# A float32 first block, and the first two blocks in one written-out order

## The chip, the core and the metric

One core of a Trainium2 chip runs the kernel. The metric is the device time of one execution in microseconds. Its engines are named as the profile names them: PE (TensorE, the matrix products), DVE (VectorE), ACT (ScalarE), POOL (GpSimd) and SP, whose queue issues nearly all DMAs.

## What is computed

A convolution with weights made for each position, then a feed-forward layer. `x` is [4, 4096, 192] float32, `weight_gen` [4, 4096, 8, 7] float32; `w_in` [192, 2048] and `w_out` [2048, 192] arrive as float64.

```python
w = softmax(weight_gen, axis=-1)
out = einsum('bshk,bskhg->bshg', w, x_unf)   # 7 taps: rows s-6 .. s
h = out.reshape(16384, 192) @ w_in
g = h * (1.0 / (1.0 + exp(-1.702 * h)))
result = (g @ w_out).astype(float32)
```

## The kernel before

**Tiles.** The 16384 rows are 32 blocks of 512 (`NB`, four tiles of 128 rows), and the 2048 columns of `w_in` are 16 slices of 128 (`NF`). One block and one slice are a **unit**; 512 units run in order. A unit's first products (`whole`, L386, and `halves`, L396) make `h` of 128 columns by 512 rows in one bank of PSUM, its gate (`gate`, L406: Tanh on ACT, a multiply on DVE) makes `g`, `split` (L412) makes two float16 parts of `g` on ACT and DVE, and its second products (`second`, L418) add to the block's output in PSUM, which `store` (L430) writes out.

**Precision.** Everything that goes into a product is split in a high and a low float16 part, so that a float32 product becomes several float16 ones: four of 512 columns in `whole`, half of one in `halves` (only 64 of the 192 inputs are left for it, so two units share the array, one in each half of its rows), and three of 192 columns for each of four row tiles in `second`. The parts need a power of two as a scale for each block (`scales`, L224) and one for each weight (`bound_in`, L343, and `bound_out`, L348), which come from the largest sum of absolute values.

**Weights.** They arrive as float64 and are narrowed to float32 in place (`narrow`, L318), 512 columns at a time: two ACT steps (bits of the low word, L326, and the exponent, L329), two DVE steps (L332, L333), and one ACT pass for the absolute sums (L337). The float32 value then stands in the high word of each 64-bit element, so it is read with a step of two words. Key `i` is the upper 128 rows of `w_in`, `t` the other 64 (two halves stacked on the partitions), `o` is `w_out`. Once a scale is there, `parts_in`, `parts_tail` and `parts_out` (L362 to L378) make the high part on ACT (L358), the low part on DVE (L360), and eight small DMAs copy the tail's high part to `th_` (L373).

**The convolution.** For the first block, `attend_first` (L169) makes seven taps and three sums on DVE, and PE turns the four results by products with an identity and adds them up in two banks of PSUM (L182, float32 products). `scales(0)` and `split_first` (L258) go from there. For all other blocks POOL makes taps and sums (`attend`, L153), DVE and ACT split (`split_x`, L271), and a DMA transposes (`turn`, L282). `hold` (L478) is a small copy on POOL that makes it wait for a DVE result.

**Order.** Every engine and queue takes its instructions in the order in which they are written. `plan` (L459) gives each step of the side work a due number counted in units, negative ahead of the first; the loop at L581 goes through the units in groups: first two, then 85 groups of six (`sixes`), and calls what is due between the units. Within a six, three units get `whole` first and three after `halves`, and the second products of the six before are spread between them (`seconds`, L563). Banks `h0` to `h5` go around by the unit's number (`bank`, L383); the four remaining uses (top sums, exponents, warm-up products, turned taps) share them. All loads are issued on SP's queue at the start (L483 to L495).

## Time and profile before

| | |
|---|---|
| median of 3 runs | 1084.66 us (1083.29 to 1085.37) |
| span of the profiled execution, first to last instruction | 1082.0 us; its own time is given by this span alone |
| PE busy | 1047.2 us, 97% of the span |
| DVE, ACT, POOL busy | 875.3, 702.7 and 721.9 us |
| mean granted PE clock | 0.984 of full speed |

Lnn is a line of the kernel above. "x" counts instructions; a float32 product stands as two records. A busy PE says only that a product was under way. Waits of engines off the path cost nothing by themselves.

### The profile page before, as it was taken

How to read it: one execution, taken by the hardware profiler on the slowest of the kernel's cores; microseconds unless marked ns; L12 is line 12 of the kernel's file. 1: busy time of each engine (PE TensorE's matmuls, PEld its weight loads, DVE VectorE, ACT ScalarE, POOL GpSimd, SP SyncE). 2: the span in 40 equal slices, each digit the busy share in tenths (PEclk: the TensorE clock that was granted, in tenths of full speed). 3: DMA queues.
4: the chain of work that ended last, by engine and by line, in shares of the span. 5: the costliest groups of instructions: out<-in, count | busy, mean ns of one | idle time of the engine just before them, and what ended most of it. 6: DMA issues, size and time to landing. Idle time of an engine off the chain costs nothing.

```text
span 1082.0 us, 22229 instructions
## 1 busy us (share of the span) xinstructions
PE 1047.2 (97%) x8821; PEld 734.4 (68%) x8821; DVE 875.3 (81%) x1558; ACT 702.7 (65%) x1251; POOL 721.9 (67%) x484
## 2 busy tenths in 40 slices
PE   5589999999999999999999999999999999999998
PEld 4156767777777767776776677667766777676766
DVE  8877878888797888878788887978887787789765
ACT  5866766666666666666666666656676666667665
POOL 4449858677855868686587868568776856886100
PEclk9689999999999999999999999999999999999999
DMA  9300220313012121301212120121212102101010
GB/s 303 128 18 17 47 78 18 92 33 93 16 36 82 25 92 33 89 18 33 78 34 92 32 84 24 33 78 32 90 36 75 33 18 92 33 22 41 18 33 16
DMA packets 73519, 60.71 MB, mean 56 GB/s; under 512 B 60620, under 2 KB 66252, under 8 KB 71880
## 3 DMA queue, kind: packets, MB, share of 16 engines
q1 hardware_dynamic: 73128, 59.11, 18.9%
q8 instruction: 69, 1.13, 0.4%
q14 instruction: 34, 0.28, 0.1%
q10 hardware_dynamic: 288, 0.20, 0.1%
HBM read 31.96 MB, written 12.58 MB: 41 GB/s over the span
## 4 chain that ended last, share of the span: by engine, by line
PE 94%; DVE 3%; ACT 2%; issue 1%; DMA 1%; SPq 0%; ACTq 0%
PE o L426 17%; PE o L428 16%; PE o L427 16%; PE h L391 10%; PE h L392 10%; PE h L393 10%; PE h L394 10%; PE h L403 6%; DMA xb<-in_x_dram 1%; DVE tap L149 0%; ACT abs L337 0%; DVE g L416 0%; ACT bits L326 0%; DVE h L410 0%; DVE m L332 0%
## 5 line engine op out<-in xcount | busy, mean ns | idle before, releaser
L426 PE MATMUL o<-wos,g 128*128 128x192 f16 x2048 | 505.4, 247 | 0.1
L428 PE MATMUL o<-woh,g 128*128 128x192 f16 x2048 | 504.7, 246 | 0.0
L427 PE MATMUL o<-wol,g 128*128 128x192 f16 x2048 | 504.7, 246 | 0.0
L410 DVE SCALAR_TENSOR_TENSOR h<-th,h 128x512 f32<-128x512 f32 x512 | 347.0, 693 | 177.9 <-ACT th L409 170.3
L409 ACT ACTIVATE th<-h,s 128x512 f32<-128x512 f32 x512 | 343.3, 687 | 219.1 <-PE h L404 125.2
L416 DVE SCALAR_TENSOR_TENSOR g<-g,h 128x512 f16<-128x512 f16 x512 | 349.4, 682 | 13.2 <-ACT g L415 1.2
L164 POOL TENSOR_TENSOR acc<-acc,prod 128x768 f32<-128x768 f32 x186 | 344.6, 1853 | 14.6
L415 ACT ACTIVATE g<-h 128x512 f16<-128x512 f32 x512 | 306.0, 598 | 46.2 <-DVE h L410 46.2
L149 POOL TENSOR_TENSOR prod<-xb,wb 128x768 f32<-128x768 f32 x186 | 291.7, 1568 | 11.1
L426 PEld LDWEIGHTS <-g 128*128 128x128 f16 x2048 | 200.5, 98 | 75.5 <-issue 35.6
L427 PEld LDWEIGHTS <-g 128*128 128x128 f16 x2048 | 200.7, 98 | 36.4
L428 PEld LDWEIGHTS <-g 128*128 128x128 f16 x2048 | 200.7, 98 | 0.1
L393 PE MATMUL h<-xt,w0h 128*128 128x512 f16 x512 | 195.1, 381 | 0.0
L391 PE MATMUL h<-xt,w0l 128*128 128x512 f16 x512 | 195.0, 381 | 0.0
L394 PE MATMUL h<-xt,wth 128*128 128x512 f16 x512 | 195.0, 381 | 0.0
L392 PE MATMUL h<-xt,w0h 128*128 128x512 f16 x512 | 195.0, 381 | 0.0
L143 POOL TENSOR_TENSOR wb<-wb,wr 128x224 f32<-128x224 f32 x31 | 17.9, 577 | 217.8 <-DVE wr L140 214.9
L278 DVE SCALAR_TENSOR_TENSOR xs<-acc,s,xs 128x512 f16<-128x512 f32 (+1 forms) x62 | 92.8, 1536 | 0.0
L393 PEld LDWEIGHTS <-w0h 128*128 128x128 f16 x512 | 50.3, 98 | 61.0 <-issue 1.1
L394 PEld LDWEIGHTS <-wth 128*128 128x128 f16 x512 | 50.3, 98 | 61.0 <-issue 1.0
L403 PE MATMUL h<-xt,tl 64*128 64x512 f16 x256 | 70.9, 382 | 2.3 <-DVE g L416 2.3
L404 PE MATMUL h<-xd,tl 64*128 64x512 f16 x256 | 71.1, 382 | 0.5 <-DVE g L416 0.5
(94 smaller groups left out, 526.2 us busy)
## 6 DMA issues: line engine op xcount, KB each, us to landing
xb<-in_x_dram SPq DMA_DIRECT2D x12, 1344.0 KB, 6.4
out_dram<-osb SPq DMA_DIRECT2D x31, 384.0 KB, 2.4
wb<-in_weight_gen_dram SPq DMA_DIRECT2D x16, 224.0 KB, 3.2
ro<-in_moe_w_out_dram SPq DMA_DIRECT2D x4, 768.0 KB, 12.3
xb<-in_x_dram SPq DMA_DIRECT2D x3, 768.0 KB, 6.2
ri<-in_moe_w_in_dram SPq DMA_DIRECT2D x4, 512.0 KB, 8.7
...
```

Source lines behind the costliest of these rows:

```text
L164: nc.gpsimd.tensor_tensor(acc, acc, t, ALU.add)
L391: nc.tensor.matmul(ps, lhsT=w0l[:, s], rhs=x0, start=start, stop=False)
L392: nc.tensor.matmul(ps, lhsT=w0h[:, s], rhs=x2, start=False, stop=False)
L393: nc.tensor.matmul(ps, lhsT=w0h[:, s], rhs=x0, start=False, stop=False)
L394: nc.tensor.matmul(ps, lhsT=th_[:, s], rhs=x1, start=False, stop=stop)
L409: nc.scalar.activation(t, hp[u], AF.Tanh, scale=scale[u[0]][:, 4:5])
L410: nc.vector.scalar_tensor_tensor(hp[u], t, 1.0, hp[u], ALU.add, ALU.mult)
L415: nc.scalar.activation(g[:, 0], hp[u], AF.Copy, scale=2.0**-12)
L416: nc.vector.scalar_tensor_tensor(g[:, 1], g[:, 0], -(2.0**12), hp.pop(u), ALU.mult, ALU.add)
L426: nc.tensor.matmul(o, lhsT=lo, rhs=wos[:, d], start=a and j % 2 == 0, stop=False, skip_group_check=True)
L427: nc.tensor.matmul(o, lhsT=hi, rhs=wol[:, d], start=False, stop=False, skip_group_check=True)
L428: nc.tensor.matmul(o, lhsT=hi, rhs=woh[:, d], start=False, stop=z, skip_group_check=True)
```

## The change

The loads, their order, and everything from the third block on (its sixes, due numbers and banks relative to the six) stay as they are. Changed is what lies ahead of it:

- **Block 0 in float32.** The turned first block is copied to SBUF as float32 (`keep`, ACT and DVE). `whole` becomes one float32 product with the narrowed weights, `halves` two of half height, `second` one for each row tile, with the narrowed `w_out` as its moving operand. `gate` writes float32 `g` to SBUF; `split` is not called for this block, and neither its scale nor its parts are made.
- **Taps of block 0.** Five on DVE, two on POOL (`dtap`, `ptap`), two sums on DVE, and five results turned (`tr`) instead of four. Both subtractions of the softmaxes 0 and 1 are on POOL. The warm-up has 11 products instead of 7; the one in front of the first products (5, float16) is gone.
- **Weights' scales and parts** are made while block 0 runs, in pieces of 1024 columns for bits, absolute sums and parts (key ending in `w`); four DMAs instead of eight copy the tail's high part.
- **One list.** All steps of the first 32 units stand in `ORDER`, which is written out as read; each name is one step of one of the functions. `W` is `whole`, `X` the half products of a group of four units, `gt` and `gm` the two steps of a gate, `gh` and `gl` those of a split, `S` the second products (a, b: two row tiles), `nb nm n1 n2 na` narrowing and sums, `ph pl ps pd` the parts, `sN.k` softmax, `aN.k` attention, `cN xN tuN` scales, split and turn of block N, `hold` POOL's waits. The units use four banks; `h4` and `h5` are left to exponents and tops. The sixes start at unit 32; units 28 to 31 get their second products in the first of them.

```diff
 ONE = float(1 << 23)
+
+ORDER = """
+warm.11 s1.0 s0.0 s1.1 s0.1 s0.2 s0.3 s0.4 s0.5 s0.6 s0.7 ptap.1 dtap.5 dtap.2 tr.5 ptap.3 dtap.6 dtap.4
+tr.6 sum.2.3 nm.i0 dtap.0 tr.2 nm.i1 sum.0.1 s1.2 nb.i0 nb.t0 tr.0 n1.i0 n2.i0 s1.3 nm.t0 tr.4 nb.i1 n1.t0
+s1.4 s1.5 n2.t0 s1.6 keep.0 keep.2 a1.0 keep.1 W.0 n1.i1 nb.i2w W.1 n2.i1 a1.1 na.i0w X.0 nm.o0 a1.1p nm.i2
+n1.i2 W.2 gt.0 a1.2 gm.0 nb.o0w W.4 gt.1 n1.o0 a1.2p W.3 gt.2 gm.1 n2.o0 W.5 gm.2 nm.o1 a1.3 S.0a gt.3 n1.o1
+S.0b nb.t1 gm.3 a1.3p n2.i2 X.1 n2.o1 s3.0 s2.0 s2.1 S.1b gt.5 a1.4 W.6 nm.t1 gm.5 nm.i3 W.7 s2.2 a1.4p gt.6
+s2.3 S.1a s2.4 gm.6 gt.7 W.9 gm.7 gt.4 s3.1 S.2 a1.5 gm.4 s3.2 na.o0w n1.i3 W.8 n1.t1 nb.o2w a1.5p S.3 n2.t1
+s3.3 na.t0w n2.i3 X.2 a1.6 s2.5 na.i2w s3.4 S.4 a1.6p nm.o2 s3.5 nm.o3 n1.o2 gt.8 W.11 n2.o2 gt.9 s2.6 lp2
+gm.8 S.5 a2.0 c1.0 gt.11 nm.o4 W.10 nb.o4w gm.11 a2.1 S.6 gm.9 n1.o4 gt.10 s3.6 W.13 n2.o4 a2.1p S.7 gm.10
+n1.o3 W.12 n2.o3 a2.2 bin.0 nm.o5 c1.1 S.8 na.o2w n1.o5 a2.2p c1.2 X.3 n2.o5 x1.0 x1.1 bin.1 S.9 gt.12 x1.2
+bin.2 tu1 W.14 ph.t0w cg1 gm.12 W.15 gt.13 pl.t0w pd.t0w S.10 ph.i0w s4.0 ph.i2w gm.13 s4.1 S.11 pl.i0w
+gt.15 xd1 s4.2 S.12 na.o4w pl.i2w gt.14 gm.15 W.16 hold.A a2.3 gm.14 W.17 bout.0 a2.3p X.4 s4.3 bout.1 W.18
+gt.17 bout.2 gt.16 W.19 a2.4 ph.o2w gm.16 S.13 gm.17 gh.16 co1 a2.4p gh.17 ps.o2w S.14a gl.17 S.14b gl.16
+ph.o0w S.15a S.15b pl.o0w ps.o0w W.20 st.a pl.o2w st.b S.16a gt.18 S.16b gt.19 S.17a hold.B gm.18 a2.5 S.17b
+gm.19 gh.18 W.21 gh.19 gl.18 a2.5p ph.o4w gl.19 S.18 ps.o4w X.5 pl.o4w W.22 gt.20 gt.21 a2.6 gm.20 W.23
+gm.21 gh.20 S.19 gh.21 gl.20 a2.6p gt.23 W.24 gt.22 gm.23 S.20 gl.21 gh.23 hold.C a3.0 gm.22 W.25 gl.23
+gh.22 S.21 s4.4 gl.22 a3.1 c2.0 X.6 W.27 gt.25 a3.1p gt.24 gm.25 W.26 gm.24 gh.25 c2.1 S.22 a3.2 gh.24 gl.25
+gt.27 c2.2 W.29 gt.26 co2 a3.2p cg2 S.23 x2.0 gl.24 gm.27 W.28 gm.26 gh.27 a3.3 S.24 gh.26 gl.27 gl.26 S.25
+x2.2 x2.1 X.7 s4.5 tu2 S.26 s4.6 gt.28 a3.3p gt.29 gm.28 W.31 gm.29 gh.28 W.30 gt.31 gl.28 a3.4 S.27 gh.29
+gm.31 gl.29 gh.31 a3.4p gt.30 gl.31 xd2 gm.30 gh.30 a3.5 gl.30 a3.5p a3.6 a3.6p
+"""
+TURNED = [a for a in ORDER.split() if a.startswith("tr.")]
...
+    def softmax(blk, eng=nc.gpsimd):
...
+        if blk == 0:
+            near["w"], near["r"] = w, r
+            return
+        yield
...
+    def weights_near(by):
...
+        if by == "dve":
+            near[by] = ps_h.tile([P, N], F32, tag="h0", name="w")[:, 0 : J * H * K].rearrange("p (n k) -> p n k", k=K)
+            nc.vector.tensor_tensor(near[by], near["w"], near["r"], ALU.mult)
+        else:
+            near[by] = x32[1][:, 0 : J * H * K].rearrange("p (n k) -> p n k", k=K)
+            nc.gpsimd.tensor_tensor(near[by], near["w"], near["r"], ALU.mult)
...
+    turned, taps, added = [], {}, []
...
+    def first_tap(k, by):
+        if k < K - 2:
...
+        taps[k] = t
+        tap(0, {"dve": nc.vector, "pool": nc.gpsimd}[by], t, k, near[by])
+
+    def add_taps(k, l):
+        nc.vector.tensor_tensor(taps[k], taps[k], taps[l], ALU.add)
...
+    def turn_tap(k):
...
+        for ps, c, n in zip(turned, (0, P), (P, C1)):
+            for j in range(J):
+                nc.tensor.matmul(
+                    ps[:n, j * P : (j + 1) * P], lhsT=taps[k][:, j, c : c + n], rhs=ident,
+                    start=start and j == 0, stop=stop, skip_group_check=True,
+                )
...
-    def split_first():
...
-        nc.scalar.activation(x1[0:C1], b[0:C1], AF.Copy, scale=s[0:C1])
-        xd[0] = tpool.tile([P, J, P], F16, tag="xd", name="xd")
-        nc.scalar.activation(xd[0][C1:P], b[0:C1], AF.Copy, scale=s[0:C1])
-        yield
-        nc.vector.scalar_tensor_tensor(x2, a, s, x0, ALU.mult, ALU.subtract)
-        nc.vector.scalar_tensor_tensor(x1[C1:P], b[0:C1], s[0:C1], x1[0:C1], ALU.mult, ALU.subtract)
+    x32 = [const.tile([P, N], F32, name=f"x32{c}") for c in range(2)]
+
+    def keep(n):
+
+
+        if n == 2:
+            nc.vector.tensor_copy(x32[1][C1:P], turned[1][0:C1])
+        else:
+            p = (P, C1)[n]
+            nc.scalar.copy(x32[n][0:p], turned[n][0:p])
...
-    def narrow(key, a, at):
...
-        nc.scalar.activation(b, low_u, AF.Relu, bias=third, scale=2.0**-29 * (1 - 2.0**-10))
-        ring = (ps_o, "o") if at % 2 else (ps_h, f"h{4 + at // 2 % 2}")
-        m = ring[0].tile([P, QC], F32, tag=ring[1], name="m")
-        nc.scalar.activation(m, f, AF.Copy, scale=2.0**-112)
-        yield
-        m = m.bitcast(I32)
-        nc.vector.scalar_tensor_tensor(m, m, 3, b, ALU.logical_shift_left, ALU.bitwise_or)
-        nc.vector.scalar_tensor_tensor(high, high, -(1 << 31), m, ALU.bitwise_and, ALU.bitwise_or)
-        yield
-
-        t = stage.tile([P, QC], BF16, tag="abs", name="abs", bufs=1)
-        nc.scalar.activation(t, f, AF.Abs, accum_out=sums[:, at : at + 1])
...
+    narrowed = {k: words(v, F32)[1] for k, v in raw.items()}
+    bits, exps = {}, {}
+    spares = itertools.cycle(("h4", "h5"))
...
+    def narrow(step, key):
...
+        k, s = cols_of(key)
+        n = s.stop - s.start
+        if step == "nb":
+            low_u, _ = words(raw[k][:, s], U32)
+            b = stage.tile([P, n], I32, tag=f"b{n}", name="bits", bufs=2)
+            nc.scalar.activation(b, low_u, AF.Relu, bias=third, scale=2.0**-29 * (1 - 2.0**-10))
+            for i in range(n // QC):
+                bits[k, s.start // QC + i] = b[:, i * QC : (i + 1) * QC]
+            return
+        if step == "na":
...
+            one = {"t": 0, "i": 1, "o": 3}[k] + s.start // (2 * QC)
+            nc.scalar.activation(wos[:, 0:n].bitcast(BF16), narrowed[k][:, s], AF.Abs, accum_out=sums[:, one : one + 1])
+            return
+        at = k, s.start // QC
+        if step == "nm":
+            m = ps_h.tile([P, QC], F32, tag=spare(), name="m")
+            nc.scalar.activation(m, narrowed[k][:, s], AF.Copy, scale=2.0**-112)
+            exps[at] = m.bitcast(I32)
+        elif step == "n1":
+            m = exps[at]
+            nc.vector.scalar_tensor_tensor(m, m, 3, bits.pop(at), ALU.logical_shift_left, ALU.bitwise_or)
+        else:
+            _, high = words(raw[k][:, s], I32)
+            nc.vector.scalar_tensor_tensor(high, high, -(1 << 31), exps.pop(at), ALU.bitwise_and, ALU.bitwise_or)
...
-        yield from bound(0, 6, e, "h3")
+        yield from bound(0, 3, e, spare)
...
-        yield from bound(6, 12, e, "o")
+        yield from bound(3, 6, e, spare)
...
-
-    def parts_in(c):
-        s = slice(c * QC, (c + 1) * QC)
-        yield from parts_of(("i", c), to_in, w0h[:, s], w0l[:, s])
-
-    def parts_tail(c):
...
+    def parts(step, key):
+
+
+        kind, s = cols_of(key)
+        f, to = narrowed[kind][:, s], to_out if kind == "o" else to_in
+        hi, lo = (t[:, s] for t in {"i": (w0h, w0l), "o": (woh, wol), "t": tail}[kind])
+        if step == "ph":
+            nc.scalar.activation(hi, f, AF.Copy, scale=to)
+        elif step == "pl":
+            nc.vector.scalar_tensor_tensor(lo, f, to, hi, ALU.mult, ALU.subtract)
+        elif step == "ps":
+            nc.scalar.activation(wos[:, s], hi, AF.Copy, scale=2.0**-12)
+        else:
+            for p0 in (0, C1):
+                to = th_[p0 : p0 + C1, 2 * s.start : 2 * s.stop].rearrange("d (q two k) -> two d q k", two=2, k=P)
+                for h in range(2):
+                    nc.sync.dma_start(to[h], hi[h * C1 : (h + 1) * C1].rearrange("d (q k) -> d q k", k=P))
...
     def bank(u):
-        hp[u] = ps_h.tile([P, N], F32, tag=f"h{(u[0] * NF + u[1]) % Q}", name="h")
+        n = u[0] * NF + u[1]
+        hp[u] = ps_h.tile([P, N], F32, tag=f"h{n % 4 if n < few else (n - few) % Q}", name="h")
...
     def whole(u, start, stop):
 
         blk, f = u
+        if blk == 0:
+            w = narrowed["i"][:, f * P : (f + 1) * P]
+            nc.tensor.matmul(hp[u], lhsT=w, rhs=x32[0], start=start, stop=stop)
+            return
...
         blk, f = u
+        if blk == 0:
+            w = narrowed["t"][:, f // 2 * P : (f // 2 + 1) * P]
+            nc.tensor.matmul(hp[u], lhsT=w[0:C1], rhs=x32[1][0:C1], start=not last_u, stop=last_u)
+            nc.tensor.matmul(hp[v], lhsT=w[C1:P], rhs=x32[1][C1:P], start=not last_v, stop=last_v)
+            return
...
     def gate(u):
 
-        t = gpool.tile([P, N], F32, tag="th", name="th", bufs=2)
-        nc.scalar.activation(t, hp[u], AF.Tanh, scale=scale[u[0]][:, 4:5])
-        nc.vector.scalar_tensor_tensor(hp[u], t, 1.0, hp[u], ALU.add, ALU.mult)
+        th[u] = t = gpool.tile([P, N], F32, tag="th", name="th", bufs=2)
+        nc.scalar.activation(t, hp[u], AF.Tanh, scale=scale[u[0]][:, 4:5] if u[0] else SIG / 2)
+        yield
+        to = hp[u]
+        if u[0] == 0:
+            to = gg[u] = gpool.tile([P, N], F32, tag="g", name="g32")
+        nc.vector.scalar_tensor_tensor(to, th.pop(u), 1.0, hp[u], ALU.add, ALU.mult)
...
     def second(u, j):
...
+        if blk == 0:
+            w = narrowed["o"][:, d]
+            nc.tensor.matmul(o, lhsT=g[:, s], rhs=w, start=a and j % 2 == 0, stop=z, skip_group_check=True)
+            return
...
-        o, s = po.pop((blk, i)), scale[blk][:, 5:6]
+        o, s = po.pop((blk, i)), scale[blk][:, 5:6] if blk else 0.5
...
-    few = len(units) % Q
+    few = 2 * NF
...
-        plan((-36.1, -35.7, -35.1, -34.6, -33.6), softmax(0, V, w_first))
...
-        plan((-36.2,), once(warm, 7, ident, P))
-        plan((-32.1, -30.4, -27.7, -25.0), attend_first(w_first))
-        plan((-24.9, -24, -23, -22, -21, -0.04, -0.03), attend(1))
-        plan((-20.5, -18.3, -17.1, -17.1), scales(0))
...
-        raw = {"t": raw_t, "i": raw_i, "o": [raw_o[:, c * QC : (c + 1) * QC] for c in range(NO)]}
-        for k, c, at, *slots in (
-            ("t", 0, 0, -28.6, -23.2, -21.6),
...
-        plan((-8.0, -7.1, -5.8), bound_in())
...
-        plan((-3.8, -2.8), parts_in(0))
...
-        plan((-2.5, -1.4), parts_tail(1))
...
-        plan((1.95, 4.6, 4.65), bound_out())
-        for c, slots in enumerate(((4.7, 5.2), (5.3, 5.8), (6.2, 6.7), (7.55, 7.9), (7.95, 8.95), (8.2, 8.96))):
...
-        plan((8.98, 10), turn(1))
...
-        for blk in range(2, NB):
...
+            elif k == "hold":
+                nc.gpsimd.tensor_copy(held, {"A": w0l[:, DFF - 8 :], "B": wol[:, 4 * QC - 8 : 4 * QC], "C": wol[:, 6 * QC - 8 :]}[n])
...
+            elif k == "W":
+                u = units[int(n)]
+                if u in hp:
+                    whole(u, False, True)
+                else:
+                    bank(u)
+                    whole(u, True, False)
+            elif k == "X":
+                four = units[4 * int(n) : 4 * int(n) + 4]
+                for u in four[2:]:
+                    bank(u)
+                for u, v in zip(four[::2], four[1::2]):
+                    halves(u, v, u in four[:2], v in four[:2])
+            elif k in ("gt", "gm"):
+                step("gate" + n, gate, units[int(n)])
+            elif k in ("gh", "gl"):
+                step("split" + n, split, units[int(n)])
+            elif k == "S":
+                u = units[int(n.rstrip("ab"))]
+                for j in {"a": (0, 1), "b": (2, 3)}.get(n[-1], range(J)):
+                    second(u, j)
...
+        for a in ORDER.split():
+            act(a)
...
-        sixes = [units[:few]] + [units[n : n + Q] for n in range(few, len(units), Q)]
-        for k, us in enumerate([None] + sixes, -1):
...
+        sixes = [units[n : n + Q] for n in range(few, len(units), Q)]
...
-            due = seconds(sixes[k - 1] if k > 2 else sixes[0] + sixes[1] if k == 2 else ())
...
+            due = seconds(sixes[k - 1] if k else units[few - 4 : few])
```

## Rows read from the trace of the kernel before

**Rows 1.** The page's 40 slices: PE's busy tenths and granted clock.

```profile
PE   5589999999999999999999999999999999999998
...
PEclk9689999999999999999999999999999999999999
```

**Rows 2.** Table by stage: busy us of each engine, PE's clock, DMA share, GB/s.

```profile
0.00:20.30 20.30, 13.48 (x78) 11.78 (x78) 18.46 (x40) 8.67 (x14) 6.58 (x19) 1.00 0.94 277
20.30:41.00 20.70, 2.37 (x7) 0.85 (x8) 17.50 (x40) 19.60 (x41) 11.77 (x7) 0.55 0.54 195
41.00:70.00 29.00, 22.93 (x99) 10.51 (x98) 25.41 (x57) 21.70 (x42) 9.54 (x10) 0.74 0.23 69
70.00:113.20 43.20, 43.20 (x379) 31.20 (x378) 32.27 (x59) 26.77 (x49) 41.55 (x27) 1.00 0.14 32
113.20:1082.00 968.80, 965.25 (x8262) 680.06 (x8260) 781.64 (x1367) 625.94 (x1108) 652.46 (x424) 1.00 0.17 49
```

**Rows 3.** Two lines up to 113.2 us (min/median/max ns); PE's timeline behind.

```profile
L391 PE MATMUL h<-xt,w0l x32: 376/379/634, 41.1 to 112.4; 128*128 128x512 f16 x32
...
L426 PE MATMUL o<-wos,g x104: 243/246/364, 55.6 to 112.1; 128*128 128x192 f16 x104
...
113.24 0.38 PE L391 MATMUL h<-xt,w0l 128*128 128x512 f16 x1
113.45 0.38 PE L392 MATMUL h<-xt,w0h 128*128 128x512 f16 x1
```

**Rows 4.** Timelines of DVE and PE: start us, us, engine, line, instruction.

```profile
33.22 0.16 DVE L340 TENSOR_REDUCE top<-sums 128x1 f32<-128x6 f32 x1 [0.94 <-ACT abs L337]
...
41.07 0.63 PE L391 MATMUL h<-xt,w0l 128*128 128x512 f16 x1
```

**Rows 5.** Timelines of DVE and PE up to 20 us.

```profile
7.65 2.68 DVE L149 TENSOR_TENSOR tap<-xb,w 128x768 f32<-128x768 f32 x3
...
4.05 3.36 PE L476 MATMUL warm<-ident 128*128 128x128 f32 x14 [4.05 <-DVE third L90]
8.66 7.95 PE L182 MATMUL tr<-ident,tap 128*128 128x128 f32 x48 [1.25 <-DVE tap L149]
16.82 2.18 PE L182 MATMUL tr<-ident,tap 128*128 128x128 f32 x16 [0.22 <-DVE tap L179]
```

**Rows 6.** Float32 passes (14.6 to 15.4 us); float16 products (200 to 1000).

```profile
L182 PE MATMUL tr<-ident,tap x8: 275/275/377, 14.4 to 15.3; 128*128 128x128 f32 x8
...
L426 PE MATMUL o<-wos,g 128*128 128x192 f16 x1604 | 395.2, 246 | 0.0
...
L392 PE MATMUL h<-xt,w0h 128*128 128x512 f16 x400 | 151.6, 379 | 0.0
```

**Rows 7.** PE's steady timeline: half-height products of two pairs.

```profile
105.61 0.38 PE L394 MATMUL h<-xt,wth 128*128 128x512 f16 x1
105.92 0.39 PE L403 MATMUL h<-xt,tl 64*128 64x512 f16 x1
...
106.15 0.38 PE L403 MATMUL h<-xt,tl 64*128 64x512 f16 x1
```

**Rows 8.** Groups by shape, 0 to 70 us: busy us, mean ns, idle.

```profile
L410 DVE SCALAR_TENSOR_TENSOR h<-th,h 128x512 f32<-128x512 f32 x10 | 6.6, 688 | 1.5 <-ACT th L409 1.5
L409 ACT ACTIVATE th<-h,s 128x512 f32<-128x512 f32 x10 | 6.5, 675 | 2.0 <-PE h L404 2.0
...
L416 DVE SCALAR_TENSOR_TENSOR g<-g,h 128x512 f16<-128x512 f16 x8 | 5.4, 684 | 1.4 <-ACT g L415 1.2
L415 ACT ACTIVATE g<-h 128x512 f16<-128x512 f32 x9 | 5.2, 595 | 1.1 <-DVE h L410 1.0
...
L333 DVE SCALAR_TENSOR_TENSOR ri<-ri,m 128x512 int32<-128x512 int32 x4 | 2.8, 688 | 0.1
```

**Rows 9.** The same view for DVE, 120 to 1000 us, 62 to 70.

```profile
L278 DVE SCALAR_TENSOR_TENSOR xs<-acc,s,xs 128x256 f16<-128x256 f32 x28 | 54.9, 1961 | 0.0
...
L278 DVE SCALAR_TENSOR_TENSOR xs<-acc,s,xs 128x256 f16<-128x256 f32 x1 | 0.5, 480 | 0.0
```

More of the change, by code (lines that the diff above doesn't have):

```diff
@@ L1 @@
+import itertools
 import math
@@ L208, in top_of @@
         yield
-        ps = (ps_h if free[0] == "h" else ps_o).tile([P, N], F32, tag=free, name="top")
+        ps = ps_h.tile([P, N], F32, tag=free(), name="top")
         nc.tensor.matmul(ps[:, 0:n], lhsT=ones, rhs=four[:, 0:n], start=True, stop=True)
@@ L313, in words @@
     def words(a, dt):
[L314 to L337 removed]
+        return tuple(a.bitcast(dt).rearrange("p (n two) -> p n two", two=2)[:, :, i] for i in range(2))
@@ new lines, in conv_attention_then_ffn, with spare, cols_of @@
+    raw = {"t": raw_t, "i": raw_i, "o": raw_o}
+    narrowed = {k: words(v, F32)[1] for k, v in raw.items()}
+    bits, exps = {}, {}
+    spares = itertools.cycle(("h4", "h5"))
+    def spare():
+        return next(spares)
+    def cols_of(key):
+        wide = key[-1] == "w"
+        c = int(key[1])
+        return key[0], slice(c * QC, (c + 1 + wide) * QC)
+    def narrow(step, key):
[23 more added lines that the diff above has]
+            nc.vector.scalar_tensor_tensor(high, high, -(1 << 31), exps.pop(at), ALU.bitwise_and, ALU.bitwise_or)
@@ L476, in warm, with run @@
             nc.tensor.matmul(ps[:, 0:cols], lhsT=w[:, 0:P], rhs=w[:, 0:cols], start=True, stop=True)
-    def hold(t):
-        nc.gpsimd.tensor_copy(held, t)
+    def run(gen):
+        for _ in gen:
+            pass
     with tc.manual_schedule():
@@ L612, in conv_attention_then_ffn @@
                 until(n + 0.25 + i)
-                gate(u)
+                run(gate(u))
                 until(n + 0.5 + i)
                 if last:
-                    split(last)
+                    run(split(last))
                 last = u
                 until(min(n + 1 + i, z - 0.4))
-            split(last)
+            run(split(last))
             until(z)
```

209 lines of the change are left out of this document (89 added, 120 removed).

## The prediction

> **What bounds the kernel now.** I began with the page's slices of the 1082.0 us: PE is busy nine tenths or more from the fourth slice on, at full clock; only the first three slices show less [rows 1]. So the steady part is a queue of products that never empties, and the change can only move what lies ahead of it. The table by stage cuts that out: up to 20.3 us the first block's inputs are made and turned; from 20.3 to 41 PE is busy 2.37 us of 20.7 while ACT is busy 19.6; from 41 to 70 PE is busy 22.93 of 29.0 at a mean clock of 0.74; then it is full [rows 2]. Next I looked for a point that both kernels pass. Up to 113.2 us exactly 32 units (blocks 0 and 1) have had their first products and 104/4 = 26 units their second ones, and the 33rd unit starts at 113.24 [rows 3]. What follows, 480 units in 80 sixes, is written the same in both kernels. So **the end is the start of the 33rd unit plus 968.8 us** (1082.0 - 113.2) before, and the question is when that unit starts after. Last, why PE idles from 20 to 41: all weights' absolute sums must be in before their common scale (the reduction at 33.22), then come the parts, and the first product of block 0 starts at 41.07 [rows 4].
>
> **The common point.** The new list has 28 units of second products done there (S.0 to S.27) instead of 26; units 28 to 31 come in the first six. Two units are 24 products of 192 columns. A 512-column product starts every 0.216 us (113.24 to 113.45, [rows 3]), so one of 192 columns takes 0.082 and the two units 1.97: **after, the end is the 33rd start + 966.8 us.**
>
> **The new start.** x still lands at 7.6, where the taps begin [rows 5]. DVE makes five taps and two sums (before seven and three), POOL makes taps 1 and 3 beside it. On DVE that is 7 x 0.89 = 6.2 us (three taps in 2.68; a sum of the same shape counted alike), so the last pair of taps is summed at 13.9. PE turns five tiles instead of four: 80 passes against 64. Its warm-up (11 products instead of 7: 3.36 x 11/7 = 5.3) ends by 9.3, and the first turn can start at 9.1, ahead of the last record's tail. 48 passes took 7.95 us with the half-clock start in them and 16 took 2.18 [rows 5], so 80 take 7.95 + 2 x 2.18 = 12.3 at worst and 5 x 2.1 = 10.5 at full clock: turned at 19.6 to 21.6, or, if the first turns overlap the warm-up's end better, not under 13.9 + 2 x 2.1 = 18.1. I take 19.6: the longer warm-up leaves no gap before the turns, so the clock should be up by then. Then one copy out of PSUM (0.7, like the Tanh of the same shape in [rows 8]): **W.0 at 20.3**, bounds 19.0 to 22.3. Columns i0 and t0 are narrowed by then: four DVE instructions after 13.9.
>
> **Block 0 in float32.** A float32 product is two records (8 records for the 4 products of the first half tile, [rows 6]). A 512-column float16 record lasts 379 ns, a 192-column one 246: 0.416 ns a column and 166 ns that all have. The float32 record of 128 columns lasts 275; less 166 this is 109 ns, 0.85 ns a column, at the same full clock. So W costs 2 x 512 x 0.85 = 0.87 us (four float16 products: 0.86, no change), and S of one unit 4 x 2 x 192 x 0.85 = 1.31 (0.98 before). X of a group is four half-height products of two passes, 0.435 each. In float16 the two halves run side by side and the next pair starts 0.22 later, with about 0.1 to change over (0.31 after the last full-height product instead of 0.216) [rows 7]. In float32 the second pass of one half can only follow its first: side by side throughout it is 4 passes (1.74), staggered 5 (2.18), one after the other 8 (3.48). I take 2.18 + 0.2 = 2.4. Block 0: 16 x 0.87 + 16 x 1.31 + 4 x 2.4 = 13.9 + 21.0 + 9.6 = **44.5 us** (bounds 41.9 and 48.8).
>
> **Block 1 in float16 up to the point.** 16 x 0.86 + 4 x (0.44 + 0.2) + 12 x 0.98 = 13.8 + 2.6 + 11.8 = **28.2 us**.
>
> **Waits of PE in between.** DVE and ACT were busy 93.6 and 76.7 us before the point (sums of the first four stages, [rows 2]). Block 0 drops 16 splits: 10.9 us of DVE, 9.5 of ACT [rows 8]. Two taps, a sum, scales and split of block 0 save DVE some 7 more, less 0.7 for a copy. That leaves about 77 us of DVE and 67 of ACT in some 97: neither bounds on average, but chains do. POOL, busy 69.4, adds two taps of block 0 and still has some 25 us free. (a) W.4 needs the first bank back: Tanh and gate, 0.68 + 0.69, behind four ACT steps for later weights, against X.0's second half and W.2: 1 us. (b) Handover: the product bin.1 stands behind X.3 on PE; then DVE's scale (six short instructions, 1.0 by the reduction's 0.16 of [rows 4]), ph.t0w, a Tanh, ph.i0w, pl.i0w, the wide steps estimated at 1.3, twice a Tanh, and the four DMAs pd.t0w on SP's queue ahead of xd1: 5.6 to 7 us, covered by S.9 to S.12 and two W (7.0): 0 to 1. If that cover failed, all of it would show. (c) bout likewise, with six ACT steps (7.3) before S.16, against 6.5 of PE work: 1. (d) Three more groups of four, each waiting for Tanh, gate, split high and low (2.6) to free its bank: 0.7 each. Together **5 us**, bounds 1 and 15. The narrowing, bits and sums themselves cost nothing here, as long as they run under block 0's 44.5 us; the four wide tail DMAs replace eight and wait for nobody but W.16.
>
> The last cover is POOL's. The split of 256 columns takes DVE 480 ns with POOL held and 1961 in the steady part [rows 9]. If all six wide pl steps paid that 1.48 us, it were 8.9 us of DVE, which has 20 to spare; three hold copies keep POOL off most of them, so I add nothing. The Trainium skill, "SBUF — State Buffer", "SBUF: two separate sides", says that a DVE instruction with two SBUF inputs and a GpSimd one lock each other out for a whole instruction. This speaks against attending on POOL under block 0; the steady row agrees with it, and if by it all six steps fell among POOL's and no PE work covered them, the sum would be 1076; the upper bound of the waits takes that in.
>
> **Sum.** 20.3 + 44.5 + 28.2 + 5 = 98.0; + 966.8 = 1064.8 of span against 1082.0. The runs' median is 2.7 above the profiled span (1.3 to 3.4 for the single runs), and I leave that as it is: **1067.5 us**, 1.6% less. Bounds: 19.0 + 41.9 + 28.2 + 1 gives 1059.6; 22.3 + 48.8 + 28.2 + 15 gives 1083.8.
>
> **Rivals.**
> Rival 1, waits and clock as before. In the stage from 41 to 70 PE lost 6.1 us idle, and at a mean clock of 0.74 about half of the 29 us ran at half clock, 7.5 us lost [rows 2]. If block 1's chains do this again, on top of my 5: + 13.6, 1081. For: the same engines hand over the same parts. Against: float32 work fills PE meanwhile, and the clock fell only after such idle times.
> Rival 2, the early start is not there: W.0 stands ready, but ACT's queue is in order and takes the bits of i2 and sums of i0 and two exponents of late columns before the first Tanh. If PE runs dry until about 30 us, + 10: 1077. Against: these are two wide steps of some 1.3 and two of 0.6, 3.8 us, and W.0, W.1 and X.0 give PE 4.1 us beside them.
> Rival 3, slower than before: S reads w_out's narrowed values in place, every second float32 word of the 64-bit originals, as its moving operand. No PE row reads so. If TensorE then takes a column at half the pace, S costs 42 instead of 21: + 21.0, 1088.5, 0.35% over 1084.7. It decides from 1.9 times on. Against: each pass already takes two cycles a column; DVE reads and writes the same stride in its usual time (the narrowing step 688 ns, the gate, without a stride, 688, [rows 8]). The Trainium skill, "SBUF — State Buffer", "Specifications (TRN2)", says that two hits in a 16-byte line give full bandwidth. By that rule this rival would not occur; no run here shows it.
>
> **Chances.** Forecast 0.72 (1060 to 1075), rival 1 0.13, rival 2 0.06, rival 3 0.07, anything else 0.02. The range 1060 to 1080 leaves out rival 3 and the far end of rival 1. A measurement can tell 0.2%, 2.2 us, from no change. Faster by more: 0.89; within: 0.03, from rival 1's upper end; slower: 0.08.
>
> **What would show it.** Right: the first float32 W at 20 to 21 us; W passes 0.43 apart, S passes 0.165; the clock full from about 12 us on; the 33rd unit at 95 to 101, and 967 us after it. Wrong, if S passes are 0.33 apart (rival 3), if PE idles over 3 us in a piece with a half-clock stretch behind it near W.16 or S.16 (rival 1), if W.0 starts late or W.4 waits long (rival 2), or if the part behind the 33rd unit grows, which I hold to be the same.

## The result, and the profile after

The changed kernel takes 1072.16 us (median of 4 runs, 1071.98 to 1072.55) against 1084.11 us: a ratio of 0.9888, interval 0.9874 to 0.9902, 12 us less. The forecast was 1067.5 us. The time lies within the range of 1060 to 1080, 4.7 us above its likeliest value. The profiled run took 1072.55 us; its span is 1070.3 us, 2.3 us less.

The page's slices of the changed kernel (26.8 us each; PE and its clock) answer to [rows 1]:

```profile
PE   7998999999999999999999999999999999999998
PEclk9999899999999999999999999999999999999999
```

PE is now busy from the second slice on. But the fourth and fifth slices, which were full before, now each have a digit 8: one in PE's row, one in the clock's. That is new, and it lies behind block 1. The table by stage shows it; its columns are the stretch, then busy time of PE, PEld, DVE, ACT and POOL, then the granted clock and the DMA share. It answers to [rows 2]:

```profile
0.00:18.90 18.90, 14.76 (x102) 13.14 (x102) 14.37 (x34) 6.52 (x10) 8.61 (x20) 1.00 0.94 284
18.90:60.60 41.70, 40.48 (x173) 26.54 (x172) 33.31 (x65) 31.74 (x52) 31.90 (x25) 1.00 0.50 162
60.60:94.60 34.00, 32.90 (x251) 22.30 (x249) 30.20 (x58) 25.57 (x41) 27.42 (x19) 1.00 0.10 24
94.60:106.30 11.70, 9.35 (x76) 5.98 (x74) 4.87 (x10) 3.09 (x6) 11.31 (x9) 1.00 0.03 7
106.30:116.60 10.30, 7.78 (x29) 4.16 (x30) 9.48 (x19) 7.31 (x14) 9.91 (x6) 0.50 0.10 39
116.60:1070.30 953.70, 950.17 (x8136) 669.46 (x8134) 767.27 (x1339) 615.23 (x1089) 636.94 (x414) 1.00 0.18 50
```

The second line is block 0 in float32: PE 40.48 of 41.70 us, where before it was busy 2.37 of 20.7 and then 22.93 of 29.0. The stage that the change was made for is full. The third line is block 1 and is full too. The 33rd unit starts at 94.65 us, against 113.24 before and 98.0 in the forecast. The fourth and fifth lines are what was not forecast: just behind that unit PE loses 2.35 us of 11.70, then 2.52 of 10.30, and those 10.3 us run at the clock's lower level.

What PE waited for there, from the timelines of PE, DVE and POOL from 98 to 111 us (start, duration, engine, line, operation; in brackets the idle time before it and what ended it):

```profile
102.21 1.80 POOL L206 TENSOR_TENSOR acc<-acc,prod 128x768 f32<-128x768 f32 x1
...
104.05 0.95 DVE L273 TENSOR_REDUCE top<-acc 128x1 f32<-128x768 f32 x1 [6.02 <-POOL acc L206]
...
107.48 0.19 PE L255 MATMUL top<-tf,ones 128*128 128x1 bf16 x1 [3.54 <-DVE g L481]
...
110.73 0.59 PE L446 MATMUL h<-xt,w0l 128*128 128x512 f16 x1 [1.33 <-DVE s L261]
```

Read from the top: POOL ends block 3's last sum at 104.01. DVE has stood for 6.02 us at the reduction that reads this sum, and the gates and splits behind the reduction in DVE's queue have stood with it. PE's next instruction, the chain's small product, needs a bank that one of these splits clears (DVE g L481 in the bracket), so PE stands for 3.54 us, then for 1.33 us at the same bank, which the chain's next DVE step (L261) still reads. In the kernel before, POOL's last sum for block 3 and the same reduction stood so:

```profile
113.76 1.81 POOL L164 TENSOR_TENSOR acc<-acc,prod 128x768 f32<-128x768 f32 x1
...
116.48 0.94 DVE L234 TENSOR_REDUCE top<-acc 128x1 f32<-128x768 f32 x1
```

Counted from the start of the 33rd unit (113.24), POOL was done after 2.33 us and DVE came to it after 3.24 us, without a wait. Now DVE is ready for it 3.38 us after that start (at 98.03), and POOL is done only after 9.36. The waits from 94 to 118 us, grouped (total, count, longest), say the same:

```profile
ACT g L479 <- DVE h L474: 7.1, 4, 5.0
DVE top L273 <- POOL acc L206: 6.0, 1, 6.0
...
PE top L255 <- DVE g L481: 3.5, 1, 3.5
```

From the 33rd unit to the end it is 1070.30 - 94.65 = 975.65 us instead of 966.8: 8.85 us more. Of these 3.54 + 1.33 = 4.87 are idle. From 106.31 to 116.55 us the clock was at half; PE worked in about 7.8 of these 10.24 us (fifth line of the table), which at full clock take 3.9. Together 8.8.

The costs of the parts answer to [rows 3]. Groups of PE up to 94.6 us (busy, mean ns of one, idle before):

```profile
L492 PE MATMUL o<-ro,g 128*128 128x192 f32 x128 | 24.3, 334 | 0.0
L442 PE MATMUL h<-x,ri 128*128 128x512 f32 x32 | 15.8, 602 | 1.2 <-DVE g L474 1.2
...
L458 PE MATMUL h<-x,rt 64*128 64x512 f32 x16 | 8.0, 617 | 0.0
L457 PE MATMUL h<-x,rt 64*128 64x512 f32 x16 | 8.0, 617 | 0.0
```

Counted from one record's start to the next one's, the 32 W records take 15.53 us (1.22 of it idle), the 128 S records 22.44, the X records 7.71: without the idle time 44.46 us, where the forecast had 44.5. One X group in PE's timeline, from its first two records to what follows it:

```profile
20.86 0.70 PE L457 MATMUL h<-x,rt 64*128 64x512 f32 x1
20.87 0.70 PE L458 MATMUL h<-x,rt 64*128 64x512 f32 x1
...
22.79 1.13 PE L442 MATMUL h<-x,ri 128*128 128x512 f32 x2
```

### The profile page after: what moved, and what is told of

Its sections match the earlier page's. It is cut to its first block, busy times and chain, and to the rows that moved or that the text cites. A ratio compares the mean times of both kernels' runs of the same rounds, so it can differ in the third digit from the quotient of the medians.

```text
span 1070.3 us, 22014 instructions
## 1 busy us (share of the span) xinstructions
PE 1055.4 (99%) x8759; PEld 741.6 (69%) x8759; DVE 859.5 (80%) x1521; ACT 689.5 (64%) x1209; POOL 726.1 (68%) x488
## 4 chain that ended last, share of the span: by engine, by line
PE 90%; DVE 4%; ACT 3%; POOL 2%; issue 1%; POOLq 0%; ACTq 0%
PE o L495 16%; PE o L497 15%; PE o L496 15%; PE h L446 10%; PE h L447 10%; PE h L449 10%; PE h L448 10%; PE h L463 5%; PE tr L231 1%; POOL acc L206 1%; POOL prod L190 1%; ACT g L479 1%; DVE g L474 1%; DVE h L474 0%; ACT wos L382 0%
## 5 line engine op out<-in xcount | busy, mean ns | idle before, releaser
L495 PE MATMUL o<-wos,g 128*128 128x192 f16 x1984 | 489.4, 247 | 0.0
L497 PE MATMUL o<-woh,g 128*128 128x192 f16 x1984 | 488.6, 246 | 0.0
L496 PE MATMUL o<-wol,g 128*128 128x192 f16 x1984 | 488.6, 246 | 0.0
L474 DVE SCALAR_TENSOR_TENSOR h<-th,h 128x512 f32<-128x512 f32 x496 | 335.9, 693 | 167.4 <-ACT th L469 159.3
L469 ACT ACTIVATE th<-h,s 128x512 f32<-128x512 f32 x496 | 332.5, 688 | 212.9 <-PE h L464 126.2
L481 DVE SCALAR_TENSOR_TENSOR g<-g,h 128x512 f16<-128x512 f16 x496 | 338.3, 683 | 12.9 <-ACT g L479 1.2
L479 ACT ACTIVATE g<-h 128x512 f16<-128x512 f32 x496 | 296.5, 598 | 51.0 <-DVE h L474 51.0
L495 PEld LDWEIGHTS <-g 128*128 128x128 f16 x1984 | 194.2, 98 | 73.8 <-issue 34.9
L496 PEld LDWEIGHTS <-g 128*128 128x128 f16 x1984 | 194.3, 98 | 35.6 <-issue 0.7
L497 PEld LDWEIGHTS <-g 128*128 128x128 f16 x1984 | 194.3, 98 | 0.0
L446 PE MATMUL h<-xt,w0l 128*128 128x512 f16 x496 | 188.7, 380 | 1.6 <-DVE s L261 1.3
L448 PE MATMUL h<-xt,w0h 128*128 128x512 f16 x496 | 188.7, 381 | 0.0
L447 PE MATMUL h<-xt,w0h 128*128 128x512 f16 x496 | 188.7, 381 | 0.0
```

Source lines behind the costliest of these rows:

```text
L446: nc.tensor.matmul(ps, lhsT=w0l[:, s], rhs=x0, start=start, stop=False)
L448: nc.tensor.matmul(ps, lhsT=w0h[:, s], rhs=x0, start=False, stop=False)
L469: nc.scalar.activation(t, hp[u], AF.Tanh, scale=scale[u[0]][:, 4:5] if u[0] else SIG / 2)
L474: nc.vector.scalar_tensor_tensor(to, th.pop(u), 1.0, hp[u], ALU.add, ALU.mult)
L479: nc.scalar.activation(g[:, 0], hp[u], AF.Copy, scale=2.0**-12)
L481: nc.vector.scalar_tensor_tensor(g[:, 1], g[:, 0], -(2.0**12), hp.pop(u), ALU.mult, ALU.add)
```

## The experiments

**Is the reduction due too early?** Block 3's scales are four steps with due times: the reduction on DVE at 32.1 units (31.8 in the kernel before), a small product on PE at 36.1, then the rest. Two runs move the reduction alone.

```
-            sc = [max(n - 12.2, few + 0.1), n - 7.9, n - 7.89, n - 7.3]
+            sc = [n - 8.0 if blk == 3 else max(n - 12.2, few + 0.1), n - 7.9, n - 7.89, n - 7.3]
```

That is a due time of 36.0 (n is 44 for block 3).

> Edit: the first step of block 3's scales (VectorE's reduction of its attention) is due at unit 36.0 instead of 32.1; nothing else. Theory A (VectorE, in order, waits there 6.0 us for GpSimd's last sum, which ends at 104.05; TensorE runs dry for 3.5 us and then has 10.2 us at half clock): the wait falls to about 1 us (unit 36 comes at 102.5 to 103), no half clock behind it, and the time to about 1064 us (1072.2 less 3.5 and 5.1). Theory B (the stall belongs to the seam between the list and the groups of six, whatever VectorE does there): within 1 us of 1072.2.

Measured: 1067.91 us (1067.81 to 1068.03), 4.25 less than the changed kernel; span 1065.6, of which 971.0 lie behind the 33rd unit (94.58). DVE's and PE's timelines of this run:

```profile
105.59 0.95 DVE L273 TENSOR_REDUCE top<-acc 128x1 f32<-128x768 f32 x1
...
107.07 0.18 PE L255 MATMUL top<-tf,ones 128*128 128x1 bf16 x1 [3.19 <-DVE tf L252]
```

DVE no longer waits, but the wait went to PE: its small product, still due at 36.1, stands in PE's queue and now waits for the later reduction itself. So the idle time is almost the old one (3.19 us in one piece; the second piece is gone), yet the clock stayed up. What was won is the clock's share and the second piece. Theory B is out; theory A's 1064 us is missed by 3.9 us, because the wait went on to PE.

The second run puts the reduction halfway, at 34.1.

```
+            sc = [few + 2.1 if blk == 3 else max(n - 12.2, few + 0.1), n - 7.9, n - 7.89, n - 7.3]
```

> Edit: the same step due at unit 34.1. Theory A: VectorE meets it at about 98.5 to 100, waits 4 to 5 us, TensorE is dry for 1 to 3 us; if the clock still falls, 1069 to 1071, if it does not, 1065 to 1067. Theory B: 1072.

Measured: 1067.99 us (1066.84 to 1069.61). This median lies between two pairs of runs: 1069.04 and 1069.61 us, with a mean clock of 0.996 and 0.998, and 1066.84 and 1066.94 us, both with 1.0. Idle time of PE, and the table by stage, of the run with 1069.04:

```profile
104.70 0.18 PE L255 MATMUL top<-tf,ones 128*128 128x1 bf16 x1 [1.57 <-DVE tf L252]
...
107.15 0.58 PE L446 MATMUL h<-xt,w0l 128*128 128x512 f16 x1 [1.39 <-DVE s L261]
94.60:106.30 11.70, 9.60 (x77) 5.99 (x75) 6.91 (x13) 6.26 (x12) 11.39 (x8) 1.00 0.12 41
106.30:116.60 10.30, 9.45 (x56) 5.80 (x56) 8.57 (x17) 4.89 (x9) 9.83 (x7) 0.67 0.10 20
```

There is less idle time here, but the clock fell for 6.8 us. The other pair, 2.1 to 2.8 us shorter at a mean clock of 1.0, shows that the same program can also pass this place without that; theory A had named both outcomes. Neither step alone is enough, since two engines wait in this chain, each in order.

**The whole chain moved.** The reduction is due at 36.0, the small product at 38.6, behind more units of W, in a bank that is free by then; all that follows it is due right behind.

```
+            d = 38.6 - (n - 7.9) if blk == 3 else 0
+            if d:
+                sc = [36.0, 38.6, 38.6 + 0.01, 38.6 + 0.02]
-            plan(sc, scales(blk, lambda: "h0"))
+            plan(sc, scales(blk, lambda d=d: "h3" if d else "h0"))
...
-            plan([n - 6.15, n - 5], turn(blk))
+            plan([sc[3] + 0.06 if d else n - 6.15, n - 5], turn(blk))
```

> Block 3's whole chain of scales is moved, not its first step alone: the reduction due at 36.0, the small product that follows it due at 38.6 behind two more units of W (in a bank that is free by then), and all that hangs on it behind that. Theory A (the 8.85 us that were lost behind the 33rd unit come from this one chain, first by TensorE's wait and then by the clock that the wait costs): neither DVE nor TensorE waits for POOL; no idle piece over 0.5 us between 94 and 117 us, clock full to the end, 33rd unit at 94.6, and 94.65 + 966.8 = 1061.5 us of span, 1064.0 us of time; up to 1 us more if the transfer of block 3's second chunk, which landed at 121.6 us in the run with the reduction at 36.0, now comes after the first product that wants it (about 120.5 us). Rival B (POOL itself is short, so the wait only moves on, to block 3's parts or the next block): an idle piece of 3 us at 117 to 123 us, time as before this edit but for the clock, 1067.5 to 1068.5 us.

Measured: **1064.26 us** (1063.95 to 1064.77), ratio to the kernel before 0.9813 (0.9800 to 0.9827), 7.9 us less than the changed kernel; span 1062.5. DVE, PE and the table by stage of this run:

```profile
105.48 0.94 DVE L273 TENSOR_REDUCE top<-acc 128x1 f32<-128x768 f32 x1
...
108.16 0.17 PE L255 MATMUL top<-tf,ones 128*128 128x1 bf16 x1
...
110.16 0.37 PE L464 MATMUL h<-xd,tl 64*128 64x512 f16 x1 [0.41 <-DVE s L261]
94.60:106.30 11.70, 11.70 (x94) 7.71 (x93) 7.78 (x13) 7.94 (x15) 11.31 (x9) 1.00 0.12 41
106.30:116.60 10.30, 9.89 (x88) 6.74 (x86) 9.51 (x19) 4.58 (x9) 9.91 (x6) 1.00 0.03 6
```

PE is full in both stages and the clock stays up. POOL's busy time there is 11.31 and 9.91 us as in the changed kernel: it is as slow as before, but nobody waits for it. From the 33rd unit (94.46) to the end it is 968.0 us, 1.2 over the forecast's 966.8. Rival B is out. This run also starts late: its first tap began at 8.04 us, held by x's transfer, against 7.40 in the changed kernel's profile.

A variant with the reduction at 35.1 and the product at 38.3 (the same edit with these two numbers):

> As the run with the product behind unit 38, but the reduction due at 35.1 and the product at 38.3, behind one unit of W of the next group instead of two. Theory A: the chain ends about 1 us earlier, so no wait for the transfer at 120 us, but DVE may wait up to 0.5 us for POOL's last sum (about 104.0 us) and TensorE up to 0.6 us for the product: within 1 us of the other, 1063.0 to 1065.0 us. Rival B: idle at 117 to 123 us, 1067 us or more.

Measured: 1065.09 us (1064.23 to 1065.7). PE stands for 1.32 us ahead of the small product at 107.49, again for a split of DVE; the clock stays up. Within the runs' spread of the other one, and no better.

**POOL's pass doubled.** In `attend`, the last tap's product of block 3 is computed twice, in the changed kernel and in the one with the chain moved.

```
                 tap(blk, nc.gpsimd, t, k, w)
+                if blk == 3 and k == K - 1:
+                    tap(blk, nc.gpsimd, t, k, w)
```

> The changed kernel, with the last tap's product of block 3 computed twice on POOL: 1.6 us more on POOL ahead of block 3's last sum, with the same result. Theory A (the chain from POOL's last sum of block 3 over DVE's reduction to TensorE is what loses the time behind the 33rd unit): all of it shows: DVE waits 7.6 us instead of 6.0 at the reduction, TensorE's largest idle piece is 5.1 us instead of 3.5, and the time is 1.6 us longer, 1073.8 us, more only if the clock stays down longer. Rival E (that wait only stands beside the true limit, which is the order of gates on ACT and DVE): idle piece and time as before, 1072.2 us.

Measured: 1072.84 us (1072.72 to 1073.05), 0.7 more than the changed kernel, not 1.6. The chain itself does what theory A says (lines are two further down in this kernel):

```profile
103.04 1.80 POOL L208 TENSOR_TENSOR acc<-acc,prod 128x768 f32<-128x768 f32 x1
...
104.87 0.95 DVE L275 TENSOR_REDUCE top<-acc 128x1 f32<-128x768 f32 x1 [7.66 <-POOL acc L208]
...
108.30 0.19 PE L257 MATMUL top<-tf,ones 128*128 128x1 bf16 x1 [5.16 <-DVE g L483]
```

DVE's wait is 7.66 (7.6 expected), PE's 5.16 (5.1 expected). In this profile the 33rd unit starts at 93.85, 0.8 us sooner than in the changed kernel's, since the 0.83 us that PE waited before 63.85 us there is absent. From the 33rd unit to the end it is 977.2 us, 1.5 us more. The missing 0.9 us of the time lie ahead of the chain, not in it.

> The same doubled pass on POOL, in the kernel with block 3's chain of scales moved behind unit 38. There POOL's last sum ended at 103.8 us and the reduction came at 105.5. Theory A: the 1.6 us fill just this slack: DVE waits 0 to 0.3 us, and the time stays at 1064.3 us within 0.5. Rival E or a POOL that is short behind it as well: 1.6 us longer, 1065.9 us or more.

Measured: 1064.39 us (1063.83 to 1066.37), against 1064.26 without the extra pass. POOL and DVE:

```profile
104.86 1.82 POOL L208 TENSOR_TENSOR acc<-acc,prod 128x768 f32<-128x768 f32 x1
...
106.71 0.96 DVE L275 TENSOR_REDUCE top<-acc 128x1 f32<-128x768 f32 x1
```

The reduction comes 0.03 us after POOL's end and has not waited. So the same 1.6 us of POOL cost 1.5 us in the one kernel behind the 33rd unit and nothing that the time shows in the other. (This profile, of the slowest of the four runs, has 968.9 us behind the 33rd unit instead of 968.0. The difference lies far behind the chain: PE waits 0.66 us for a transfer before 287.34 us, as it waits 0.68 us before 288.62 in the run with the reduction due at 36.0, where no pass is doubled.) Rival E is out.

**The hold copies left out.** Three small copies keep POOL off until a wide pl step of DVE is done. Without them (`hold.A`, `hold.B` and `hold.C` deleted from the list):

> Edit: the three small GpSimd copies that make it wait for the low parts of the weights are left out; the reduction stays due at 32.1. Theory A: GpSimd gets block 3 done about 6.5 us sooner (its waits of 2.4 and 4.4 us), at 97 to 98, VectorE's wait at the reduction is gone, and the time is about 1064 to 1067, if low parts beside GpSimd cost TensorE up to 3 us in front of unit 32. Theory C (the two engines shut each other out for whole instructions, so that both get slower): the six wide low parts take 2.5 us or more instead of 1.2, unit 32 starts 3 us or more later than 94.65, and the time is 1069 or more.

Measured: 1074.43 us (1073.05 to 1075.12), 2.3 more. The 33rd unit starts at 97.12. DVE's wide steps from 40 to 80 us, first of this run, then of the changed kernel (mean ns of one behind the comma):

```profile
L421 DVE SCALAR_TENSOR_TENSOR wol<-ro,sc,woh 128x1024 f16<-128x1024 f32 x3 | 5.1, 1712 | 1.2 <-ACT woh L419 1.2
L421 DVE SCALAR_TENSOR_TENSOR w0l<-ri,sc,w0h 128x1024 f16<-128x1024 f32 x2 | 3.8, 1924 | 0.0
```

```profile
L421 DVE SCALAR_TENSOR_TENSOR wol<-ro,sc,woh 128x1024 f16<-128x1024 f32 x3 | 4.2, 1427 | 1.2 <-ACT woh L419 1.2
L421 DVE SCALAR_TENSOR_TENSOR w0l<-ri,sc,w0h 128x1024 f16<-128x1024 f32 x2 | 2.5, 1280 | 0.0
```

Beside POOL a w0l step takes 0.64 us longer and a wol step 0.29; POOL pays too. Its first tap beside them:

```profile
58.09 2.57 POOL L190 TENSOR_TENSOR prod<-xb,wb 128x768 f32<-128x768 f32 x1
...
93.62 0.57 POOL L174 TENSOR_TENSOR wb<-wb,wr 128x224 f32<-128x224 f32 x1 [6.75 <-DVE wr L168]
```

An undisturbed tap takes 1.54. And the start that POOL gains is lost again, 6.75 us, at a step of the next softmax that needs DVE; in the changed kernel it waits 1.35 us there. DVE's wait at the reduction stays what it was:

```profile
106.50 0.95 DVE L273 TENSOR_REDUCE top<-acc 128x1 f32<-128x768 f32 x1 [5.96 <-POOL acc L206]
```

So theory A's gain is not there, and the holds alone are not what makes POOL late; they save about 2 us of DVE's wide steps. Theory C named the right time (1069 or more), at too high a price for a step (2.5 us or more). What dates POOL's last sum is visible in both traces: DVE's part of the softmax of block 4 (`s4.5` in the list) comes 4.0 us ahead of the 33rd unit, at 90.68 us in the changed kernel and at 93.13 here, and the POOL step that waits for it (at 91.16 and 93.62) begins 12.85 us of work without a longer gap, up to the end of that sum. No run moved `s4.5`, so what this would give is open.

**The warm-up.** With 7 products instead of 11 (`warm.7`):

> Edit: 7 warm-up products instead of 11, as before the change. Theory D (the longer warm-up closes the gap ahead of the turns, so that the clock is up when they start, at 7.3 in the profile against 12.0 before): the turns run at half clock until about 12, the first block's first product starts at 20 to 21 instead of 18.94, and the time grows by 1 to 2 us. Rival: the last turn waits for VectorE's sums either way, and nothing moves (0.3 us).

Measured: 1072.64 us (1071.22 to 1073.8), which is no difference that this measurement tells. In the profile the clock rose at 13.68 us instead of 7.32, W.0 came at 21.37 instead of 18.94 and the 33rd unit at 96.22, 1.6 us later (PE's 0.83 us wait before 63.85 us is absent here). Behind it the stretch at half clock was 6.8 us instead of 10.24, but PE waits once more, 0.52 us ahead of 774.21 us, and from the 33rd unit to the end it is 975.3 us, only 0.3 less. So the profiled run, the slowest of its four, is 1.25 us longer than that of the changed kernel. Theory D holds for the start of the first block; a gain in the time is not shown, since the runs of the two kernels overlap.

**The first gate ahead.** On top of the moved chain, the first gate's Tanh and product go ahead of later weights' steps.

```
-X.0 nm.o0 a1.1p nm.i2 n1.i2 W.2 gt.0 a1.2 gm.0 nb.o0w
+X.0 gt.0 nm.o0 a1.1p nm.i2 W.2 gm.0 n1.i2 a1.2 nb.o0w
```

> As the run with the product behind unit 38, and the first gate's two steps put ahead of three steps of the weights' parts on ACT and one on DVE. Theory A: W.4 starts when the first gate's DVE step ends, about 24.0 us instead of 25.14: the idle piece of 1.2 us ahead of it goes, and the time falls by 0.7 to 1.2 us against that run, 1062.8 to 1063.3 us where that one is at 1064.0. Rival C (block 0 is bound by the words that ACT and DVE make, not by this wait): the same piece comes back ahead of a later unit of block 0, and the time is the same within 0.4 us.

Measured: 1064.22 us (1063.78 to 1065.43), no gain. The wait before W.4 is gone and comes back one W later (the bracket's idle time; first the run with the chain moved, then this one):

```profile
25.75 2.85 PE L442 MATMUL h<-x,ri 128*128 128x512 f32 x6 [1.19 <-DVE g L474]
```

```profile
26.91 1.13 PE L442 MATMUL h<-x,ri 128*128 128x512 f32 x2 [0.87 <-DVE g L474]
```

W.0 to the 33rd unit takes 74.88 us in the one and 74.81 in the other. Rival C holds: a wait taken away at the head of a full queue of gates turns up at the next gate.

**All taps on DVE.** One part of the change undone, on top of the moved chain (`ptap.1`, `ptap.3` become `dtap.1`, `dtap.3`):

> The kernel with the chain moved, and one part of the change undone: taps 1 and 3 of block 0 on DVE again instead of POOL. DVE's taps take 0.89 us each, in a row without gaps, so the last pair of taps is summed 1.8 us later, the turns end 1.8 us later if they follow DVE, and so do W.0 (20.7 to 21.4 us) and the end: theory T (the start of block 0 is set by DVE's taps), 1066.0 us. Rival F (the turns on TensorE, 10.6 us for 80 passes in a row, set it): W.0 less than 0.5 us later, 1064.3 to 1064.8 us. POOL also gets its next work 3.1 us earlier in its queue, but that work waits for DVE, so no gain from that is expected.

Measured: 1065.16 us (1065.15 to 1065.17), 0.9 more. W.0 comes 12.89 us behind the first tap (7.40 to 20.29), against 11.54 in the other (8.04 to 19.58): 1.35 us, between the two theories. PE's turns, first of the run with the chain moved, then of this one:

```profile
9.05 10.60 PE L231 MATMUL tr<-ident,tap 128*128 128x128 f32 x80 [0.36 <-DVE tap L190]
```

```profile
9.27 2.41 PE L231 MATMUL tr<-ident,tap 128*128 128x128 f32 x16 [0.17 <-DVE tap L190]
```

The first turn starts 1.87 us behind the first tap instead of 1.01, since tap 1 now stands ahead of tap 5 in DVE's queue: 0.86 us. The turns then take 11.09 us (to 20.36) instead of 10.60. Of these 0.5 us, 0.19 is one more wait for DVE. For the rest there is a cause that is not the edit: the clock rose at 9.79 us, inside the turns, and at 8.11, ahead of them, in the other profile. (In the run with the reduction due at 36.0, with the unedited taps, it rose at 9.71 and the turns took 10.88.) So DVE sets about 1 us of the 1.35.

**The price of the 8-byte step.** Block 0's second products read their moving operand from flat words instead of every second one.

```
-            w = narrowed["o"][:, d]
+            w = x32[0][:, 0:D]
```

> The second products of block 0 take their moving operand from the first 192 columns of the turned x, which lie side by side, and not from the high words of the weights' pairs, which lie 8 bytes apart; so block 0's part of the output isn't computed, and no second product waits for the weights' words. Theory S (the 8-byte step costs nothing, four products of 192 columns take what float32 takes): a unit of S stays at 1.33 to 1.36 us. Rival D (the step costs a part of the pass): 1.28 to 1.30 us, which is 0.05 to 0.08 us less for each of 16 units, about 1 us in all; were the step to halve the rate it would be under 1.0 us. The time itself may fall by up to 2 us, since S.0 and its fellows no longer wait for words.

Measured: 1070.82 us in the single run. The S records up to 94.5 us, in this run and (shown above) 24.3 and 334 in the changed kernel:

```profile
L492 PE MATMUL o<-x,g 128*128 128x192 f32 x128 | 23.3, 329 | 0.0
```

From start to start 21.45 us instead of 22.44, 1.34 a unit instead of 1.40. Inside a unit the records of this run start 162.5 ns apart, those of the changed kernel 170.5. The step costs 1.0 us for 128 records, 5%; halving is out. The 1.34 lies in the range that theory S named, and outside rival D's 1.28 to 1.30, but both had taken the unit in the changed kernel too short; the difference between the kernels, 0.06 us a unit, is what rival D expected.

## Why the prediction was right, and where it was off

**The start** was forecast at 20.3 us and came at 18.94. The turns did not wait for a slow clock: it rose at 7.32 us, not at 12, and the 80 passes, begun at 8.41 beside DVE's taps, took 10.60 us, where 10.5 was the estimate at full clock. They ended at 19.01, so the 19.6 was too late by 0.6 us. The other 0.7 is the copy out of PSUM, which the forecast put behind the turns:

```profile
18.03 0.59 ACT L306 COPY x<-tr 128x512 f32<-128x512 f32 x1 [1.57 <-PE tr L231]
```

ACT copies the first bank while PE still turns into the second, and W.0 follows the last turn without a wait.

**Block 0** was forecast at 44.5 and took 44.46, by errors that cancel: X took 1.93 a group instead of 2.4 (the two halves start 0.01 us apart and run side by side throughout, the ideal case that I had named as 1.74 before the changeover), S 1.40 a unit instead of 1.31 (the step of 8 bytes, 0.06, and changeovers), and the W took 14.3 us together instead of 13.9. That the sum came out to 0.1 us is luck. **Block 1** took 29.0 instead of 28.2 (W 14.2 instead of 13.8, X 2.2 instead of 2.6, S 12.4 for 12 units instead of 11.8).

**The waits of PE before the 33rd unit** were forecast at 5 us and came to 2.28: 1.22 before W.4 (a, 1 forecast), 0.83 at bout.1 (c, 1 forecast), 0.23 in a group, where (d) had 2.1, and nothing at the handover (b). The wait of 0.83 is not in every run: eight of the other profiles do not have it. Sum: 18.94 + 44.46 + 29.0 + 2.28 = 94.7, where the forecast had 98.0 and a range of 95 to 101.

**The step that failed** is the last: that the part behind the 33rd unit is the same, 966.8 us. It took 975.65 us, and the forecast had itself named a growth there as a sign of being wrong. That the time came within 4.7 us of the forecast is in part luck: the 33rd unit came 3.35 us early, which hides that much of the 8.85 us lost behind it. The instructions there are the same, but their inputs are not as early as before. The forecast put POOL down as having "some 25 us free" and looked no further. POOL does block 1's, 2's and 3's attention in a stretch that is now 18.6 us shorter, and waits in it for DVE, by the holds and by the next softmax; its last sum for block 3 ends at 104.0, when DVE has wanted it since 98.0. The runs with the chain moved and with POOL's pass doubled show that this chain is the cause: 7.9 us come back when nobody stands in it. Had the forecast taken the due times of the steady part as needs with a date, and asked when POOL meets each, it would have found the wait. With the 33rd unit where it came, the rest as forecast would have given 94.65 + 966.8 + 2.3 = 1063.8 us. The run with the chain moved, at 1064.26 us and with 968.0 behind the 33rd unit, shows that the 966.8 holds to 1.2 us once nobody stands in this chain.

**The rivals.** Rival 1 (waits with a half clock behind them) came true in kind but at another place, behind the 33rd unit instead of near W.16 or S.16, and with 8.85 us instead of 13.6. Rival 2 did not occur: W.4 waited 1.2 us. Rival 3 did not: the step costs 5% of S, not 100%. The Trainium skill, "SBUF — State Buffer", "Specifications (TRN2)", says that two hits in a 16-byte line give full bandwidth, and that each cross to a new line pays a penalty. The trace agrees in that the rate is not halved; whether the 1.0 us for 128 records is the price of the lines, of which words 8 bytes apart touch twice as many, no run here shows.

**POOL beside DVE's wide steps** was added at nothing, with the holds as the cover, and 8.9 us if that cover were gone. The run without holds shows about 2.1 us (2 x 0.64 and 3 x 0.29), and the 33rd unit 2.1 us later behind W.0 (77.84 us instead of 75.71; 3.0 against the profiles without the 0.83 us wait, which have 74.8 to 74.9). The Trainium skill, "SBUF — State Buffer", "SBUF: two separate sides", says that such instructions lock each other out; the trace agrees in direction, since both are longer (w0l 1924 ns instead of 1280, POOL's tap 2.57 us instead of 1.54), at a price well below the one that the steady row gave.
